# Backward attention by half sequences, early weight loads, a shared ring for the weight gradients, and one head of four of dS transposed on TensorE

## The chip, the cores and the metric

The kernel runs on one core of one Trainium2 chip. The metric is the device time of one execution in microseconds (us), the median of the timed runs. Where runs counted as slow (over 1.5% above the fastest of the same kernel), they are left out of the ratios.

Engines are called PE (TensorE matmul), PEld (its weight loads), DVE (VectorE), ACT (ScalarE), POOL (GpSimd) and SP (SyncE, used here only to issue DMAs). A name with a q, as in SPq, is that engine's DMA-issuing instructions. "PEclk" is the granted TensorE clock, 1.00 at full speed.

## The reference, cut to what matters

Forward and gradient of four residual layers over 2048 tokens of width 640: linear attention (A), sliding-window attention (B), A, B. Both have 32 heads of 20 channels. All A layers share weights, and all B layers do, so the weight gradients sum over two layers each.

```python
def _B_ref(x, wqkv, wo):
    B, S, D = x.shape
    H = 32; Dh = D // H; W = 256
    ...                                   # q, k, v from x @ wqkv
    scores = jnp.einsum("bhqd,bhkd->bhqk", q, k) * (Dh ** -0.5)
    mask = (idx[:, None] - idx[None, :] >= 0) & (idx[:, None] - idx[None, :] < W)
    p = _softmax(jnp.where(mask[None, None], scores, -1e9), axis=-1)
    o = jnp.einsum("bhqk,bhkd->bhqd", p, v)
    return (...)(o) @ wo                  # heads put back side by side

x = A_x
x = x + _A_ref(_layernorm(x), A_wqkv, A_wo)
x = x + _B_ref(_layernorm(x), B_wqkv, B_wo)
x = x + _A_ref(_layernorm(x), A_wqkv, A_wo)
x = x + _B_ref(_layernorm(x), B_wqkv, B_wo)
# outputs: x, and the gradients of A_x, A_wqkv, A_wo, B_wqkv, B_wo for a given grad_out
```

## The kernel before

The stages run one after another: forward; the first output gradient dO ("first dO"); backward attention of layer 3; then "B-to-A" (through layer 3's projections down into layer 2) and "A-to-B" (layer 2 into layer 1); the same three for layers 1 and 0; at last the weight gradients.

Backward attention works on units. A unit is one of 8 groups of four heads and one of 16 blocks of 128 queries, with up to three blocks of 128 keys. The order of PE's work is written by hand: step s of the loop works on parts of several units, so that PE need not wait for the exponential (ACT) and the product dS (DVE) of the unit just issued. dS has to be transposed for dq, which runs eight units later. All DMA transposes are issued by SP, the slab loads (q, k, v and dO of one head group) by ACT, and the stores by SP.

```python
def dma(self, out, in_, eng=None): (eng or self.nc.scalar).dma_start(...)   # ACT unless told (abridged)
def st(self, out, in_): self.dma(out, in_, self.nc.sync)                    # SP
def ld(self, out, in_): self.dma(out, in_, self.nc.gpsimd)                  # POOL
def tr(self, out, in_): self.nc.sync.dma_start_transpose(out=out, in_=in_)  # SP

def seg_attention_bwd(self, l):
    LAG = 8
    units = [(g, b) for g in range(G) for b in range(TT)]
    ...
        psl = self.pool(st, "atl", 2)          # slabs: this head group and the next
        pe = self.pool(st, "ate", 9)           # e, ds, dsT of nine units
        ps_sp = self.pool(st, "pss", 3, PSUM)  # three score buffers
        ps_o = self.pool(st, "pso", 2, PSUM)   # two accumulators
        ...
        def dscore(u, half, ps):
            ...                                # ds = score * e, two heads of four at a time, on DVE
            if half == 1:
                dsT_of[u] = pe.tile([P, 12, P], BF, name="dsT")
                self.tr(dsT_of[u][:, 0:4 * nkt, :], ds_of[u][:, 0:4 * nkt * P])   # all four heads
        ...
        for s in range(n + LAG):
            if s < n and units[s][1] == 6 and units[s][0] + 1 < G:
                load(units[s][0] + 1)          # seven slabs of 512 KB
            if s < n:
                expo(s, 0, scores(s, 0, "QT", "KT"))              # scores of heads 0, 1
            if 0 <= s - 3 < n:
                dscore(s - 3, 1, scores(s - 3, 1, "dOT", "VT"))   # dS scores of heads 2, 3
            key_products(s)                                       # dV and dK
            if s < n:
                expo(s, 1, scores(s, 1, "QT", "KT"))
            if 0 <= s - 2 < n:
                dscore(s - 2, 0, scores(s - 2, 0, "dOT", "VT"))
            if 0 <= s - LAG < n:
                dq(s - LAG)

def seg_B_to_A(self, l, acc, dqT):
    ...
        WT = self.load_w(pW, 1, "WT")     # DMA transposes of the weights, in each B-to-A
        WoT = self.load_w(pW, 0, "WoT")

def weight_grads(self, ls, out_dW, out_dWo):
    ...
        for kind, (srcs, width, dst) in enumerate(((self.hn_d, 480, out_dW), (self.o_d, HD, out_dWo))):
            with ExitStack() as s2:
                pW = self.pool(s2, "wg")          # left operands: closed and opened anew per kind
                pw = self.pool(s2, "wgw", 2)
                ...                               # load lhs of two layers, then rhs by columns, then matmuls
```

The softmax here doesn't subtract the row's maximum and nothing guards it: scores larger than these inputs give would overflow.

## Time and profile before

| | before |
|---|---|
| time | 2887.16 us, median of 2 (2881.89 and 2892.43) |
| profiled span | 2894.6 us, mean granted clock 0.757 |
| attention, layers 3 and 1, first to last exponential | 400.3 and 382.5 us |
| wait of PE before each B-to-A | 40.4 and 40.8 us |
| idle of PE before and within the weight gradients | 23.9 + 61.9 us |

The first view is the part of the profile page that cuts the span into 40 slices of 72 us, here of the kernel before. A digit is a busy share (or the clock) in tenths.

```profile
PE   7588997489987676778397996876866978896796
PEclk9789897688876655555598995555558979898898
DMA  6699884498884999999944669999995355835624
```

Where PEclk reads 5 and DMA reads 9, the kernel is in backward attention: slices 15 to 19 and 25 to 30, counted from 1 (slice 20 is mostly PE's wait before B-to-A). PE is never full there although it is the engine with the most work.

The next view gives busy times in chosen stretches of the kernel before: first the two attention stages, then the four holes of the weight gradients. The columns are the stretch, its length, busy us of PE, PEld, DVE, ACT and POOL with counts, the granted clock, the DMA share (the packets' time over the time of the 16 DMA engines; it passes 1 where packets overlap) and GB/s.

```profile
978.50:1378.70 400.20, 305.08 (x4172) 116.18 (x4171) 244.97 (x310) 228.84 (x375) 146.25 (x238) 0.50 1.12 201
1753.70:2136.20 382.50, 306.50 (x4173) 116.09 (x4171) 244.45 (x310) 229.28 (x375) 146.25 (x238) 0.50 1.13 211
2449.00:2473.00 24.00, 0.15 (x2) 0.00 (x0) 2.08 (x6) 1.45 (x3) 0.00 (x0) 0.61 1.04 324
2605.00:2625.00 20.00, 0.44 (x3) 0.00 (x0) 0.66 (x1) 0.00 (x0) 0.00 (x0) 0.58 0.96 353
2670.00:2692.00 22.00, 0.55 (x5) 0.18 (x2) 0.49 (x1) 0.00 (x0) 0.00 (x0) 0.57 0.96 355
2824.00:2845.00 21.00, 0.50 (x3) 0.21 (x3) 0.66 (x1) 0.00 (x0) 0.00 (x0) 0.56 0.98 352
```

In attention PE is busy for 305 of 400 us, at half clock throughout. In the holes PE does nothing while 352 to 355 GB/s arrive (324 in the first).

The view of waits of the kernel before, for PE, says for whom it stood: total us, times, longest.

```profile
PE acc L806 <- DMA dsT<-ds: 79.7, 29, 11.7
PE d L581 <- DMA WT_32780<-in_B_wqkv_dram: 40.8, 1, 40.8
PE d L581 <- DMA WT_21469<-in_B_wqkv_dram: 40.4, 1, 40.4
PE wg L971 <- DMA wg_r_36633<-dqkvT_117: 23.9, 1, 23.9
PE wg L971 <- DMA wg_r_37765<-dqkv_115: 21.6, 1, 21.6
```

The first line is the transposed dS arriving late. The timeline of the kernel before shows one such wait. PE (start, length, work, and in brackets the idle time before it and who ended it):

```profile
1187.79 0.50 PE L731 MATMUL sp<-KT,QT 32*128 32x384 bf16 x2
1187.80 0.50 PE L731 MATMUL sp<-VT,dOT 32*128 32x384 bf16 x2
1199.95 0.30 PE L806 MATMUL acc<-dsT,ksl 128*32 128x128 bf16 x4 [11.65 <-DMA dsT<-ds]
```

and, of the same view and kernel, SP's queue around it:

```profile
1154.78 2.67 SPq L136 DMA_TRANSPOSE dsT<-ds  x1
1157.54 4.02 SPq L127 DMA_DIRECT2D dqkvT_117<-dqkvT_g  x7
1161.66 38.98 SPq L136 DMA_TRANSPOSE dsT<-ds  x10
```

SP issues ten transposes back to back over 38.98 us, 3.9 us each, and dq waits.

Unit paces, worked out from the starts of the exponentials in the trace (us per unit, b = 0 to 15, then the sum), show where a group of heads loses time. This is head group 4 of layer 3, before:

```
2.9 2.6 2.1 5.8 14.2 5.0 1.5 4.5 1.5 2.8 2.6 2.6 2.6 4.1 2.3 2.4   = 59.4
```

Quiet units, those without a stall, take 2.6 us; this is called the quiet pace below. Units b = 3 to 7 stall. The middle groups take 48 to 59 us (layer 3) and 46 to 57 us (layer 1), the first and last 37 to 40 us.

### The profile page before, as it was taken

The page shows a single profiled execution, that of the slowest core. Times are in us where ns is not written, and L with a number is a line of the kernel's source. Part 1 is how long each engine was busy: PE and PEld are TensorE (multiplying, and loading weights), DVE is VectorE, ACT ScalarE, POOL GpSimd, SP SyncE. Part 2 cuts the span into 40 slices and gives each one's busy share as a digit, 9 for nine tenths or more (in the row PEclk, how much of TensorE's full clock was granted, in tenths as well). Part 3 has the DMA queues.
Part 4 walks back from the last instruction along what each step waited for, and adds up shares of the span by engine and source line. Part 5 has one row for each costly group of instructions (what it writes and reads, how often), then busy time and mean ns, then how long its engine had stood idle before and what let it go on. Part 6 is the DMA issues. An engine that isn't in the chain of part 4 may idle for free. (4 is left out here: it accounts for less than half of the span.)

```text
span 2894.6 us, 60635 instructions
## 1 busy us (share of the span) xinstructions
PE 2261.8 (78%) x24412; PEld 1255.8 (43%) x24412; DVE 1335.5 (46%) x2804; ACT 1297.4 (45%) x2339; POOL 852.0 (29%) x1310
## 2 busy tenths in 40 slices
PE   7588997489987676778397996876866978896796
PEld 5345554245544332233265762332324756344344
DVE  6445553344324665566285675664754845000000
ACT  4257676146765555556143665654642545000000
POOL 0124444125545433333243233332442311000000
PEclk9789897688876655555598995555558979898898
DMA  6699884498884999999944669999995355835624
GB/s 199 206 173 186 176 178 126 141 182 172 178 187 119 243 210 202 178 209 180 197 153 121 165 171 227 218 205 184 226 191 164 122 137 179 197 74 188 220 73 159
DMA packets 1001434, 507.72 MB, mean 175 GB/s; under 512 B 841920, under 2 KB 964800, under 8 KB 1000128
## 3 DMA queue, kind: packets, MB, share of 16 engines
q1 hardware_dynamic: 793152, 240.60, 47.2%
q10 hardware_dynamic: 194816, 216.04, 25.3%
q0 software_dynamic: 13184, 47.20, 5.4%
q8 instruction: 191, 3.13, 0.4%
q14 instruction: 91, 0.75, 0.1%
HBM read 173.41 MB, written 148.50 MB: 111 GB/s over the span
## 5 line engine op out<-in xcount | busy, mean ns | idle before, releaser
L764 DVE TENSOR_TENSOR ds<-sp,e 128x768 bf16<-128x768 f32 (+2 forms) x512 | 460.6, 907 | 315.3 <-PE sp L731 285.3
L745 ACT ACTIVATE e<-sp 128x768 bf16<-128x768 f32 (+2 forms) x512 | 389.2, 774 | 185.8 <-PE sp L731 166.8
L359 ACT ACTIVATE e<-s 128x768 bf16<-128x768 f32 (+2 forms) x512 | 373.9, 774 | 148.0 <-PE s L357 106.6
L749 POOL TENSOR_SCALAR_AFFINE_SELECT e<-e 128x512 bf16<-128x512 bf16 x256 | 163.1, 637 | 520.0 <-ACT e L745 272.9
L731 PE MATMUL sp<-KT,QT 32*128 32x384 bf16 (+2 forms) x1024 | 243.1, 477 | 57.7 <-ACT e L745 28.9
L362 POOL TENSOR_SCALAR_AFFINE_SELECT e<-e 128x512 bf16<-128x512 bf16 x256 | 163.4, 638 | 414.1 <-ACT e L359 410.7
L731 PE MATMUL sp<-VT,dOT 32*128 32x384 bf16 (+2 forms) x1024 | 245.3, 470 | 44.9 <-DVE ds L764 28.0
L975 DVE CAST wg_r<-wg 128x480 bf16<-128x480 f32 (+1 forms) x36 | 21.7, 602 | 417.0 <-PE wg L971 417.0
L977 ACT CAST wg_r<-wg 128x480 bf16<-128x480 f32 (+1 forms) x24 | 12.4, 515 | 422.8 <-PE wg L971 403.9
L806 PE MATMUL acc<-dsT,ksl 128*32 128x128 bf16 x2880 | 125.0, 304 | 84.0 <-DMA dsT<-ds 79.7
L357 PE MATMUL s<-ring 32*128 32x128 bf16 x2880 | 168.3, 236 | 26.2 <-ACT e L359 25.0
L583 ACT ACTIVATE dh_junk<-d 128x320 bf16<-128x320 f32 x128 | 56.2, 439 | 240.1 <-PE d L581 240.0
L365 POOL TENSOR_SCALAR_AFFINE_SELECT e<-e 128x512 bf16<-128x512 bf16 x224 | 143.9, 642 | 0.0
L581 PEld LDWEIGHTS <-dqkvT 128*128 128x128 bf16 x960 | 93.1, 100 | 116.4 <-issue 81.6
L357 PEld LDWEIGHTS <-ring 32*128 32x128 bf16 x2880 | 84.2, 98 | 135.9 <-issue 128.7
L753 POOL TENSOR_SCALAR_AFFINE_SELECT e<-e 128x512 bf16<-128x512 bf16 x224 | 142.8, 637 | 0.0
L731 PEld LDWEIGHTS <-dOT 32*128 32x128 bf16 x1024 | 76.9, 99 | 149.5 <-issue 145.0
L231 PEld LDWEIGHTS <-ln_hnT 128*128 128x128 bf16 x960 | 96.5, 107 | 92.4 <-DMA ln_hnT<-ln_hn 34.6
L218 DVE TENSOR_TENSOR car<-d,car 128x320 bf16<-128x320 f32 x128 | 62.2, 486 | 158.4 <-PE d L216 157.8
L378 PEld LDWEIGHTS <-e 128*128 128x128 bf16 x2880 | 103.8, 98 | 67.1 <-POOL e L365 37.1
L806 PEld LDWEIGHTS <-ksl 128*32 128x32 bf16 x2880 | 61.9, 121 | 163.1 <-issue 112.0
L731 PEld LDWEIGHTS <-QT 32*128 32x128 bf16 x1024 | 55.0, 100 | 177.1 <-issue 174.6
(774 smaller groups left out, 4608.1 us busy)
## 6 DMA issues: line engine op xcount, KB each, us to landing
qkvT_127<-ring ACTq DMA_DIRECT2D x16, 768.0 KB
qkvT_131<-ring ACTq DMA_DIRECT2D x16, 768.0 KB
dqkvT_117<-dqkvT_g SPq DMA_DIRECT2D x96, 80.0 KB
dqkvT<-dqkvT_117 POOLq DMA_DIRECT2D x4, 1920.0 KB, 14.1
dqkvT_116<-dqkvT_g SPq DMA_DIRECT2D x96, 80.0 KB
dqkvT<-dqkvT_116 POOLq DMA_DIRECT2D x4, 1920.0 KB, 13.5
dqkv_115<-dkv_t SPq DMA_DIRECT2D x16, 320.0 KB
dqkv_114<-dkv_t SPq DMA_DIRECT2D x16, 320.0 KB
```

Source lines behind the costliest of these rows:

```text
L231: nc.tensor.matmul(ps, lhsT=hnT[:, k, :], rhs=W[:, k, ci * HD:(ci + 1) * HD], start=(k == 0), stop=(k == self.DT - 1))
L357: nc.tensor.matmul(ps[:, j, i * P:(i + 1) * P], lhsT=ring[r0:r0 + HP, G + g, kt * P:(kt + 1) * P], rhs=ring[r0:r0 + HP, g, qs], start=True ...
L359: nc.scalar.activation(ev[:, 2 * half:2 * half + 2], ps[:, :, 0:nkt * P].rearrange("p h (i q) -> p h i q", q=P), ACT.Exp, scale=self.c_att)
L362: nc.gpsimd.affine_select(out=ev[:, :, nkt - 1, :], in_=ev[:, :, nkt - 1, :], compare_op=ALU.is_ge, fill=0.0, base=0, pattern=[[0, 4], [1, ...
L365: nc.gpsimd.affine_select(out=ev[:, :, 0, :], in_=ev[:, :, 0, :], compare_op=ALU.is_ge, fill=0.0, base=-1, pattern=[[0, 4], [-1, P]], chan ...
L378: nc.tensor.matmul(ov[:, (g % 4) * 4 + hh, :], lhsT=ev[:, hh, i, :], rhs=slabs[(k0 + i) % len(slabs)][:, c0:c0 + DH + 1], start=(i == 0), ...
L731: nc.tensor.matmul(ps[:, j, 0:nkt * P], lhsT=slabs[g][ta][r0:r0 + HP, b * P:(b + 1) * P], rhs=slabs[g][tb][r0:r0 + HP, k0 * P:(k0 + nkt) * P],
L745: nc.scalar.activation(ev[:, 2 * half:2 * half + 2], ps[:, :, 0:nkt * P].rearrange("p h (i k) -> p h i k", k=P), ACT.Exp, scale=c_att)
L749: nc.gpsimd.affine_select(out=ev[:, :, nkt - 1, :], in_=ev[:, :, nkt - 1, :], compare_op=ALU.is_ge, fill=0.0, base=0, pattern=[[0, 4], [-1 ...
L753: nc.gpsimd.affine_select(out=ev[:, :, 0, :], in_=ev[:, :, 0, :], compare_op=ALU.is_ge, fill=0.0, base=-1, pattern=[[0, 4], [1, P]], chann ...
L764: nc.vector.tensor_tensor(out=dv[:, hs], in0=ps[:, :, 0:nkt * P].rearrange("p h (i k) -> p h i k", k=P), in1=ev[:, hs], op=ALU.mult)
L806: nc.tensor.matmul(acc[HP * hh:HP * (hh + 1), j * P:(j + 1) * P], lhsT=tok("k", g, k0 + i, hh), rhs=dsT[:, hh * nkt + i, :], start=(i == 0 ...
```

## The change

Four things are intended:

1. Attention: slabs by half sequences (half as large, in a ring of three), one head of four of dS transposed on PE instead of by DMA, and a new order of PE's work to make room for it. The key products move behind the second scores.
2. WT and WoT for both B-to-A stages are transposed once, early, and kept.
3. The weight gradients' operands go through two shared rings (6 left tiles, 8 right tiles of half a sequence) that last over all four gradients. The first left tiles are loaded before the last A-to-B.
4. The copy of dK moves from DVE to ACT.

The diff also changes smaller things: ds and dsT have 8 and 7 buffers instead of 9, a score matmul that crosses the half-sequence boundary is split in two, and in the weight gradients SP instead of ACT issues the loads and the output projection comes first.

The diff, cut to its core (half-slab indexing and the rest of the weight-gradient code are cut):

```diff
-            psl = self.pool(st, "atl", 2)
-            pe = self.pool(st, "ate", 9)
+            psl = self.pool(st, "atl", 3)
+            po = self.pool(st, "ato", 2)
+            pe = self.pool(st, "ate")
 ...
-                    self.tr(dsT_of[u][:, 0:4 * nkt, :], ds_of[u][:, 0:4 * nkt * P])
+                    self.tr(dsT_of[u][:, 0:3 * nkt, :], ds_of[u][:, 0:3 * nkt * P])
+
+            def flip(u):
+                nb = span(units[u][1])[1]
+                tp = ps_o.tile([P, 1024], BF, name="acc")
+                for i in range(nb):
+                    nc.tensor.transpose(tp[:, i * P:(i + 1) * P], ds_of[u][:, (3 * nb + i) * P:(3 * nb + i + 1) * P],
+                                        self.ident)
+                dst = dsT_of[u][:, 3 * nb:4 * nb, :].rearrange("p i q -> p (i q)")
+                nc.vector.tensor_copy(dst, tp[:, 0:nb * P])
 ...
-                    nc.vector.tensor_copy(o, acc)
+                    nc.scalar.copy(o, acc)
 ...
             for s in range(n + LAG):
-                if s < n and units[s][1] == 6 and units[s][0] + 1 < G:
-                    load(units[s][0] + 1)
+                if pX is not None and s == TT:
+                    late = self.rinv[3][:, TT - 1, 0:1]
+                    self.WT_B = self.load_w(pX, 1, "WT", late)
+                    self.WoT_A = self.load_w(pX, 0, "WoT", late)
+                if s < n:
+                    g, b = units[s]
+                    if b == 2 and g > 0:
+                        load(g, 1)
+                    elif b == HT and g + 1 < G:
+                        load(g + 1, 0)
                 if s < n:
                     expo(s, 0, scores(s, 0, "QT", "KT"))
                 if 0 <= s - 3 < n:
                     dscore(s - 3, 1, scores(s - 3, 1, "dOT", "VT"))
-                key_products(s)
+                if 0 <= s - 4 < n:
+                    flip(s - 4)
                 if s < n:
                     expo(s, 1, scores(s, 1, "QT", "KT"))
                 if 0 <= s - 2 < n:
                     dscore(s - 2, 0, scores(s - 2, 0, "dOT", "VT"))
+                key_products(s)
                 if 0 <= s - LAG < n:
                     dq(s - LAG)
 ...
-            WT = self.load_w(pW, 1, "WT")
-            WoT = self.load_w(pW, 0, "WoT")
+            WT, WoT = self.WT_B, self.WoT_A
 ...
                 self.seg_B_to_A(l, acc, dqT)
+                if l == 1:
+                    right.close()
+                    pl = self.pool(right, "wgl", 6, side="right")
+                    lhs = self.wg_lhs((3, 1), 1, pl)
                 self.seg_A_to_B(l - 1, acc, dqT)
-        self.weight_grads((3, 1), self.out_dWB, self.out_dWoB)
-        self.weight_grads((2, 0), self.out_dWA, self.out_dWoA)
+        with right, ExitStack() as st:
+            pr = self.pool(st, "wgr", 8)
+            pw = self.pool(st, "wgo", 4)
+            pps = self.pool(st, "ps", 6, PSUM)
+            self.weight_grads((3, 1), 1, self.out_dWoB, lhs, pr, pw, pps)
+            self.weight_grads((3, 1), 0, self.out_dWB, self.wg_lhs((3, 1), 0, pl), pr, pw, pps)
+            self.weight_grads((2, 0), 1, self.out_dWoA, self.wg_lhs((2, 0), 1, pl), pr, pw, pps)
+            self.weight_grads((2, 0), 0, self.out_dWA, self.wg_lhs((2, 0), 0, pl), pr, pw, pps)
```

## The prediction

> **What bounds the kernel now (before, 2894.6 us span).** Stages from the windows view:
>
> - The two backward-attention stages (978-1402 and 1754-2158 us, 423 and 405 us) run at a granted TensorE clock of 0.50 throughout, PE busy 75-78%, DMA share 1.11. In quiet stretches one unit (a head group and a query block) takes 2.60 us: the timeline shows PE back to back (score pairs 0.5 us, dq 0.51, a key product 0.83). In six of eight head groups the units around b = 4-7 take 5-14 us, because PE waits for dS transposes (waits: "acc <- DMA dsT<-ds", 80 us over the kernel, single waits to 12 us). A middle group takes 46-59 us instead of about 38.
> - In 1130-1140 us the DMA records show 4096-byte slab-load packets taking 0.79 of the 16 engines; transposes (256-byte packets) fall to about 100 packets/us from 500-600. The Trainium skill, "DMA: Bandwidth & Descriptors", section on queues, rings and completion order, says each engine round-robins between queues by packet; this agrees.
> - Before each B-to-A stage PE stands 40.4 and 40.8 us, last released by the transposed weight WT.
> - Weight gradients (2449-2895 us) are a critical PE chain of 356 us with four holes of 20-24 us waiting for operands.
>
> **What the change does, costed.**
>
> 1. *Weight-gradient ring.* Operands load ahead, and the first left operands during A-to-B. The first hole shrinks to perhaps 15 us (2.6 MB must still land when the pool frees); the other three to about 6 us, because only two of four left tiles can be prefetched. Gain about 50 us. The 5.2-7.8 MB of early loads precede A-to-B's own weight transpose in the SP queue: about +8 us there.
> 2. *Early WT/WoT, once instead of twice.* The B-to-A start then waits for the dqkvT load (issued 6 us after the stage, 14 us to land): gain about 12 us each, 24 us. But the instruction order puts WT (75 blocks, about 16 us of transposing, as at 1402 us) on the SP queue in front of the WoT that the first dO stage waits for: that stage starts about 12 us later. They are not loaded during attention, as the code suggests. Net 12 us.
> 3. *Attention.* A quarter fewer transpose bytes, and loads as twice as many halves in 2 KB packets. Per middle group I estimate DMA work: transposes 38 -> 28 us, loads 14 us, stores 4 us: 55 -> 46 us. Most dsT waits should go. Against it PE gains three 128-column transposes per unit (0.106 us each at clock 0.5, plus a change of tiling mode: 0.35-0.45 us), at a place where the exp-to-dS loop leaves no slack: quiet pace 2.60 -> about 2.95 us, or 46-48 us a group, now also for the first and last groups (38 us before). DVE (a 384-column copy instead of half a 256-column one, net about +0.3 us a unit) and ACT stay below PE. "TensorE: Matmul & The Clock Gate", Part 4, says transposes do not count as activity, so I expect the clock to stay 0.50. Net: layer 3 about 20 us faster, layer 1 about 3 us.
>
> Sum: -50 +8 -12 -24 = about -80 us.
>
> **Predicted: 2807 us, 2735-2865 (8 in 10). Faster by over 2%: 0.70; within 2%: 0.26; slower: 0.04.**
>
> **What would show it.** Groups even at 45-50 us, PE busy near 95% in attention, unit pace 2.9-3.0 us, dsT waits below 25 us; attention stages 395-410 us each; first PE wait before B-to-A about 25-30 us; the first dO matmul about 12 us later; weight-gradient stage near 395 us.
>
> **What would make it wrong.** The clock rising above 0.50 in attention (large gain); flips, key products and dq sharing two PSUM buffers, so that PE waits for DVE and ACT copies (pace 3.2 us, attention slower); transposes still starving; early loads delaying A-to-B more.

## The result, and the profile after

The kernel after takes 2784.93 us, median of 2 runs (2777.49 and 2792.37). The ratio to the kernel before is 0.964, with a 95% interval from 0.958 to 0.971. Ratios in this document are the mean time of one kernel's fast runs over the mean of the other's of the same rounds, so they are not quite the ratio of the medians quoted. The profiled execution has a span of 2790.4 us at a mean clock of 0.776.

Lengths of the stages, worked out from the first and last matmuls and exponentials of each in the two traces:

| stretch | before | after | difference | predicted |
|---|---|---|---|---|
| start to the first dO matmul | 915.0 | 935.9 | +20.8 | +12 |
| attention layer 3, first to last exponential | 400.3 | 369.6 | -30.7 | -20 |
| its end to the first B-to-A matmul | 54.6 | 38.8 | -15.8 | -12 |
| attention layer 1 | 382.5 | 383.4 | +0.9 | -3 |
| its end to the first B-to-A matmul | 53.6 | 37.2 | -16.4 | -12 |
| gap before the last A-to-B | 39.2 | 48.6 | +9.4 | +8 |
| gap before the weight gradients | 23.9 | 9.6 | -14.3 | together -50 |
| PE idle within the weight gradients | 61.9 | 2.5 | -59.4 | |
| all else (PE's work in the weight gradients -7.6, small gaps elsewhere +8.9) | | | +1.3 | 0 |
| sum | | | -104.1 | -80 (rounded) |

PE's waits in the kernel after, from the same view as before (total, times, longest):

```profile
PE sp L752 <- ACT e L767: 40.5, 41, 5.5
PE d L588 <- DMA dqkvT<-dqkvT_116: 23.6, 1, 23.6
PE d L588 <- DMA dqkvT<-dqkvT_117: 23.2, 1, 23.2
PE d L545 <- DMA WoT_14005<-in_B_wo_dram: 22.5, 1, 22.5
PE wg L1039 <- DMA wg_r<-in_grad_out_dram: 9.6, 1, 9.6
```

No wait for a DMA of dsT is among the lines of this view any more. Before B-to-A PE now waits 23 us for the operand dqkvT instead of 40 us for the weight. A new wait of 22.5 us stands in the first dO stage, and one of 9.6 us is what remains before the weight gradients.

The same stretches as before in the kernel after: two attention stages, the gap before the weight gradients, the weight gradients.

```profile
1002.50:1372.00 369.50, 333.08 (x4622) 157.67 (x4622) 254.82 (x373) 252.10 (x434) 145.68 (x238) 0.54 0.99 187
1737.50:2120.90 383.40, 341.86 (x4622) 160.29 (x4622) 255.07 (x373) 252.84 (x435) 145.68 (x238) 0.51 0.97 179
2426.40:2436.10 9.70, 0.05 (x2) 0.05 (x2) 2.08 (x6) 1.45 (x3) 0.00 (x0) 0.62 0.50 143
2436.10:2787.10 351.00, 348.51 (x1920) 187.90 (x1920) 21.02 (x35) 12.33 (x24) 0.00 (x0) 1.00 0.62 173
```

The weight gradients are now solid: PE is busy 348.5 of 351.0 us at full clock. In attention PE is busy for 90% and 89% of the stage, and the clock is a little above 0.50.

The new wait of the first dO stage is a matter of the order in SP's queue. The timeline of SP, before:

```profile
909.26 3.69 SPq L136 DMA_TRANSPOSE WoT_14005<-in_B_wo_dram  x1
```

and after:

```profile
906.00 22.43 SPq L136 DMA_TRANSPOSE WT_15398<-in_B_wqkv_dram  x1
928.65 4.16 SPq L136 DMA_TRANSPOSE WoT_14005<-in_B_wo_dram  x1
```

The early WT, which the code asks for at step 16 of the attention loop, has reached SP's queue ahead of the WoT that the first dO stage needs. The value it is made to wait for (the reciprocal row sums of layer 3) is ready at that time, so the gate holds nothing back.

The left operands do the same to the last A-to-B. Its transpose of WT in SP's queue, before and after:

```profile
2330.29 12.39 SPq L136 DMA_TRANSPOSE WT_34858<-in_A_wqkv_dram  x1
2299.48 21.66 SPq L136 DMA_TRANSPOSE WT_36799<-in_A_wqkv_dram  x1
```

It takes 9.3 us longer, behind and beside four loads of left operands, and the transposes of v that PE waits for stand behind it.

Before the weight gradients, after the change, PE ends at 2426.4 us and starts again at 2436.1 us. SP's queue in between:

```profile
2425.40 5.16 SPq L127 DMA_DIRECT2D out_dram<-car  x2
2431.04 1.03 SPq L127 DMA_DIRECT2D wg_r<-in_grad_out_dram  x2
```

The first load of a right tile is issued 4.6 us into the gap, after the last two stores of the stage before, and PE starts 5.0 us later.

Unit paces of head group 4, layer 3, after (compare with the line of before):

```
2.5 3.1 3.0 3.5 3.6 2.3 2.3 3.0 3.0 2.9 3.0 3.0 3.0 3.0 3.0 2.8   = 46.8
```

Quiet units are slower than before (3.0 against 2.6), but none stalls in this group. In others small stalls are left at b = 1 and b = 9, just where the loads of another half slab stand in the program (the code asks for them at b = 2 and b = 8): up to 5.8 and 8.1 us in layer 1.

### The profile page after: what moved, and what is told of

It reads as the page before. It is cut to its first block, busy times and chain, and to the rows that moved or that the text cites. A ratio compares the mean times of both kernels' runs of the same rounds, so it can differ in the third digit from the quotient of the medians.

```text
span 2790.4 us, 63430 instructions
## 1 busy us (share of the span) xinstructions
PE 2321.5 (83%) x25388; PEld 1342.6 (48%) x25388; DVE 1356.2 (49%) x2932; ACT 1347.3 (48%) x2467; POOL 849.7 (30%) x1312
## 5 line engine op out<-in xcount | busy, mean ns | idle before, releaser
L366 ACT ACTIVATE e<-s 128x768 bf16<-128x768 f32 (+2 forms) x512 | 374.1, 774 | 151.7 <-PE s L364 106.1
L1039 PE MATMUL wg<-wg_r,wg_l 128*128 128x480 bf16 (+1 forms) x1920 | 348.5, 345 | 12.1 <-DMA wg_r<-in_grad_out_dram 9.6
L1039 PEld LDWEIGHTS <-wg_l 128*128 128x128 bf16 x1920 | 187.9, 98 | 172.6 <-issue 10.2
L1043 DVE CAST wg_o<-wg 128x480 bf16<-128x480 f32 (+1 forms) x36 | 21.7, 602 | 335.9 <-PE wg L1039 332.0
L588 PE MATMUL d<-WT_15398,dqkvT 128*128 128x320 bf16 x960 | 144.2, 305 | 46.8 <-DMA dqkvT<-dqkvT_116 23.6
L1045 ACT CAST wg_o<-wg 128x480 bf16<-128x480 f32 (+1 forms) x24 | 12.3, 514 | 339.5 <-PE wg L1039 303.1
L588 PEld LDWEIGHTS <-dqkvT 128*128 128x128 bf16 x960 | 92.8, 99 | 81.9 <-issue 47.3
```

The source lines that it names most:

```text
L366: nc.scalar.activation(ev[:, 2 * half:2 * half + 2], ps[:, :, 0:nkt * P].rearrange("p h (i q) -> p h i q", q=P), ACT.Exp, scale=self.c_att)
L588: nc.tensor.matmul(ps, lhsT=dT[k], rhs=WT[:, k, cs], start=(k == 0), stop=(k == self.QTT - 1))
L1039: nc.tensor.matmul(ps, lhsT=lhs[i][:, tt, m * P:(m + 1) * P], rhs=rhs[i][:, tt, :], start=(i == 0 and tt == 0), stop=(i == len(parts) - 1 ...
```

## The experiments

Twelve kernels were run, each with one profile and three rounds beside the kernel before on the same chip. All gave correct results, the three with useless work included. The kernel before had a median of 2894.5, 2876.0, 2870.0 and 2892.2 us in the four calls. It differs by chip, so totals are compared by the ratio.

Stage lengths are each from a single profile. How far they can be trusted is seen where the attention code is the same: after, experiment 3 and experiment 4 have 369.6, 379.0 and 368.3 us in layer 3, and 383.4, 375.0 and 373.3 us in layer 1. Differences of 10 us between single stages are therefore not read as effects unless a second sign goes with them. A kernel named "after minus" or "before plus" is that kernel with the edit shown and nothing else.

The theory at the start was the one predicted: the PE transposes cost the slower quiet pace, and fewer DMA transposes take the stalls away. The rivals: the new order of PE's work does one or both; or half slabs do.

### 1. After, without the PE transposes

```diff
-                    self.tr(dsT_of[u][:, 0:3 * nkt, :], ds_of[u][:, 0:3 * nkt * P])
+                    self.tr(dsT_of[u][:, 0:4 * nkt, :], ds_of[u][:, 0:4 * nkt * P])
 ...
-                if 0 <= s - 4 < n:
-                    flip(s - 4)
```

> The changed kernel with the PE transposes undone: all four heads of dS go through the DMA again, the half-sequence slabs stay. Theory A (the DMA work per group was the bound of the old attention stage, and the PE transposes pay for themselves by taking a quarter of it away): quiet pace back at 2.6 us a unit, but middle groups back at 49-54 us with dsT waits, first and last groups 38 us; each attention stage, first exp to last exp, 375-395 us. Theory B (the smaller, earlier slab loads did the work, and the PE transposes cost): quiet pace 2.6 us, middle groups 40-44 us, stage 330-345 us. On the clock: if the PE transposes are what lifts the granted clock above 0.50 for stretches of the changed kernel's attention, it is 0.50 throughout here; if slab loads or order did it, the stretches at 1.0 stay.

Measured: 2817.57 us, ratio 0.971 (0.963 to 0.979). Attention takes 385.7 and 395.4 us, middle groups 48 to 54 us, and the quiet pace is still about 3.0 us. The stretches of the two stages:

```profile
997.30:1383.00 385.70, 285.23 (x4274) 130.38 (x4274) 224.67 (x250) 244.42 (x434) 146.02 (x238) 0.50 1.08 208
1745.70:2141.00 395.30, 285.77 (x4274) 130.66 (x4274) 224.91 (x250) 243.82 (x434) 146.03 (x238) 0.50 1.09 203
```

PE has 48 and 56 us less work than in the kernel after (285 against 333 and 342 us), and yet the pace is the same. PE's waits of this run say why:

```profile
PE sp L752 <- ACT e L767: 156.1, 176, 5.2
```

This line was 40.5 us after and 37.0 us before (51 times). With the key products moved behind the second scores, PE reaches those scores earlier than the exponential frees their buffer. The transposes in the kernel after fill time that would otherwise be this wait. So the cause I gave for the pace of 3.0 us is wrong: the order sets it, as experiment 5 confirms. PE's waits for dsT, 79.7 us before, are 7.9 us in this run, although all four heads are on DMA.

### 2. Before, with the PE transposes, their order and the dK copy on ACT

```diff
+ flip(), called as in the kernel after; DMA transposes of three heads; dK copy on ACT
-                key_products(s)
+                if 0 <= s - 4 < n:
+                    flip(s - 4)
                 if s < n:
                     expo(s, 1, scores(s, 1, "QT", "KT"))
                 if 0 <= s - 2 < n:
                     dscore(s - 2, 0, scores(s - 2, 0, "dOT", "VT"))
+                key_products(s)
```

> The kernel before with only the PE transposes of one head of four (and the dK copy on ACT and the order of PE that belong to them); full-sequence slabs, no ring, no early weights. Theory A: quiet pace 3.0 us, dS transposes 28 us a group instead of 38, so stalls at b = 4-7 shrink but do not vanish, because the 4 KB slab packets still crowd the transposes out: middle groups 48-53 us, stage about 385-395 us. Theory B (loads are everything): stalls as before on top of a 3.0 us pace, middle groups 57-62 us, stage about 430 us. Clock: stretches above 0.50 should appear here too if the transposes cause them.

Measured: 2869.36 us, ratio 0.987 (0.980 to 0.995). Attention takes 374.1 and 369.3 us; quiet pace 3.0 us, middle groups 45.1 to 48.7 us. This is with whole slabs. The kernel after has 369.6 and 383.4 us, so its half slabs bring nothing to attention that these profiles show.

### 3. After, with gates that hold the early loads back

```diff
             WoT = self.load_w(pW, 1, "WoT")                       # in the first dO stage
+            self.WT_B = self.load_w(pX, 1, "WT", WoT[:, 0, 0:1])
+            self.WoT_A = self.load_w(pX, 0, "WoT", WoT[:, 0, 0:1])
 ...
             WT = self.load_w(pW, 0, "WT")                         # in the last A-to-B
+            if pl is not None:
+                self.lhs0 = self.wg_lhs((3, 1), 1, pl, WT[:, 0, 0:1])
```

Each early load now has to follow the weight that the running stage needs, by a copy of one element of that weight into its target.

> The changed kernel with two loads put behind the ones that are needed first: WT_B and WoT_A wait for the WoT of the first dO stage, and the left operands of the weight gradients wait for A-to-B's WT. Theory: the 20.8 us delay of the first dO matmul and the 9.4 us longer start of the last A-to-B stage are both queueing on the DMA behind transfers nobody needs yet. First dO matmul back at about 915 us (from 936), gap before the last A-to-B stage back at about 39 us (from 48.6), all else unchanged: 28-30 us faster than the changed kernel, about 2755 us. Rival (the DMA is simply full there, so the order does not matter): the time comes back within the first dO stage or at the start of the weight gradients, total gain under 10 us.

Measured: 2773.67 us, ratio 0.956 (0.949 to 0.962). The first dO matmul comes at 911.3 us, 24.6 us earlier than after. The gap before the last A-to-B shrinks by 10.3 us to 38.3 us, but that stage grows from 98.5 to 112.0 us. The gate on the weight works. The one on the left operands only moves their cost.

The start of a run varies by chip and run, so the first dO matmul is best judged over all runs. In the five kernels with the order of before it came at 904 to 918 us (mean 911.1), in the five with the order of after at 923 to 936 us (mean 929.5), and in the four with the gate at 910 to 917 us (mean 912.1).

### 4. After, with rings of four

```diff
-                    pl = self.pool(right, "wgl", 6, side="right")
+                    pl = self.pool(right, "wgl", 4, side="right")
 ...
-            pr = self.pool(st, "wgr", 8)
+            pr = self.pool(st, "wgr", 4)
```

Four left and four right tiles are one gradient's operands, so nothing can be prefetched for the next one.

> The changed kernel with the rings cut to one set: 4 right tiles instead of 8 and 4 left tiles instead of 6, so nothing loads ahead across a boundary. Theory (the gain of 74 us in the weight-gradient part is loading ahead): holes of 8-20 us return at the three boundaries between products and, as there is now only one set of right tiles, smaller ones at each column block: stage 40-90 us longer than the changed kernel's 361 us. Rival (the gain comes from the new order, out-projection first, and the early left operands): stage within 15 us of 361 us.

Measured: 2842.11 us, ratio 0.980 (0.972 to 0.987). PE idles 66.1 us within the weight gradients, as before the change (61.9), and the time from the last A-to-B matmul to the last weight-gradient matmul is 430.6 us against 360.7 us after. So the prefetching is the gain, not the half tiles, the shared pool, the new order of the gradients or the loads from SP by themselves, all of which this run keeps. The first gap is 4.7 us here against 9.6 us.

### 5. Before, with only the key products moved

```diff
                     dscore(s - 3, 1, scores(s - 3, 1, "dOT", "VT"))
-                key_products(s)
                 if s < n:
                     expo(s, 1, scores(s, 1, "QT", "KT"))
                 if 0 <= s - 2 < n:
                     dscore(s - 2, 0, scores(s - 2, 0, "dOT", "VT"))
+                key_products(s)
```

All four heads still go through DMA.

> The kernel before with one edit: the key products of a step are issued on PE after the second pair of score matmuls instead of before it. No PE transposes, no halves. New theory C (formed after the run without PE transposes kept the 3.0 us pace): the pace of the changed kernel is set by the order of PE, not by the transposes, because nothing is left to fill the 1.4 us between a score matmul and the dS matmul that needs its PSUM buffer. Then quiet pace goes from 2.60 to 3.0 us here, with PE waiting for ACT's exp before the dS matmul many times. Rival (the dK copy on ACT or the split matmuls slowed it): pace stays 2.60 us. The stage total should move less than the pace (400 and 383 us before), since it was held by DMA.

Measured: 2866.67 us, ratio 0.995 (0.990 to 1.000). In its profile attention takes 378.4 and 367.8 us, about as in experiment 2; quiet pace 2.9 to 3.0 us, and the middle groups are 47.3 us, flat, but for one stall of 14.6 us. PE waits once for dsT, against 79.7 us in 29 waits before:

```profile
PE acc L806 <- DMA dsT<-ds: 10.2, 1, 10.2
```

The two stages of this run:

```profile
972.60:1350.90 378.30, 284.36 (x4148) 126.31 (x4146) 245.26 (x310) 223.75 (x374) 145.74 (x238) 0.50 1.10 214
1724.60:2092.40 367.80, 284.12 (x4148) 126.38 (x4146) 245.45 (x310) 224.01 (x374) 145.74 (x238) 0.50 1.09 220
```

This refutes the step of the prediction that put the DMA work of a group at 55 us for four heads: here it fits into 47.3 us. The estimate had been taken from a queue that was backed up. It also shows that most stalls go without any transpose on PE.

One caution. Experiment 5 ran on a chip on which the kernel before is faster too (2876.0 us), and its profiled run was the fastest of four (2851 us; the others 2862 to 2874). By the timed ratio the order alone gained 0.5%, by stage lengths 37 us. Experiment 2 gained 1.3% and 39 us. The two intervals overlap (0.990 to 1.000, and 0.980 to 0.995). Whether the PE transposes add up to about 1% of their own in this structure is therefore not settled.

### 6. After, with the key products back and the transposes last

```diff
-                if 0 <= s - 4 < n:
-                    flip(s - 4)
+                key_products(s)
                 if s < n:
                     expo(s, 1, scores(s, 1, "QT", "KT"))
                 if 0 <= s - 2 < n:
                     dscore(s - 2, 0, scores(s - 2, 0, "dOT", "VT"))
-                key_products(s)
                 if 0 <= s - LAG < n:
                     dq(s - LAG)
+                if 0 <= s - 4 < n:
+                    flip(s - 4)
```

> The changed kernel with PE's order put back (key products before the second pair of scores, then dq) and the PE transposes last in the step, so that they lie between dq and the next scores. Theory C: the transposes then sit in the wait for exp and cost nothing: quiet pace 2.6-2.65 us, first and last groups 37-39 us instead of 43-44 for the last, middle groups 44-47 us (now DMA, which I put at about 46 us), attention stages 340-360 us each against 370-383, total 2740-2765 us. Rival (PE time itself is the bound, so the transposes' 0.4 us adds wherever they stand): quiet pace 3.0 us, total within 10 us of the changed kernel.

Measured: 2723.08 us, ratio 0.945 (0.940 to 0.949), against 0.964 for the change itself. Attention takes 352.1 and 342.9 us, quiet pace about 2.77 us, middle groups 43 to 49 us. The key products are again between the two scores, so the exponential has time to finish; the pace is 0.17 us above that of before, where theory C had at most 0.05. The clock was at full for 47.7 and 74.1 us of the two stages.

### 7. After, with the slab loads issued by POOL

```diff
-                    self.dma(r[n], sv["qkvT"][:, i * G + g, h * HT * P:(h + 1) * HT * P])
+                    self.ld(r[n], sv["qkvT"][:, i * G + g, h * HT * P:(h + 1) * HT * P])
 ...   (the same for the other slabs)
```

The question was what stalls the kernel after at b = 1 and b = 9. ACT's timeline of the kernel after shows a suspect: a slab load stands in ACT's instruction stream and waits, and the exponential behind it comes 6 us late.

```profile
1951.57 0.81 ACT L767 ACTIVATE e<-sp 128x768 bf16<-128x768 f32 x1 [0.22 <-PE sp L752]
1958.08 0.33 ACTq L127 DMA_DIRECT2D KT<-qkvT_127  x1
1958.45 0.81 ACT L767 ACTIVATE e<-sp 128x768 bf16<-128x768 f32 x1 [6.08 <-DMA dsT<-ds]
```

> The changed kernel with the slab loads of attention issued by POOL instead of ACT. Theory D (the residual stalls of 2-5 us at b = 1 and b = 9 are ACT's queue standing at a slab load that waits for a buffer or for a DMA semaphore it shares with the transposes, so that exp comes late): these units fall to 3.0-3.5 us, ACT waits on dsT DMAs from 13-16 us a stage to under 3, middle groups 45.5-46.5 us, stages about 360-365 us, total 15-25 us less than the changed kernel. Rival (the stalls are late dS transposes, slowed by the slab packets whoever issues them): the stalls stay within 20% or move to PE waiting for dsT, total within 8 us.

Measured: 2749.33 us, ratio 0.956 (0.951 to 0.961). The units b = 1 and b = 9 of the middle groups are at 2.4 to 3.0 us, these groups at 43.2 to 48.6 us, attention 358.3 and 360.6 us. ACT's waits for dsT in the two stages go from 13.6 and 16.3 us to at most 0.6 us. The theory holds: the stalls were loads that waited in ACT's stream. (The first groups are longer than after, 43.6 and 40.9 against 37.5 us, with new stalls in them that were not looked into.) The Trainium skill, "DMA: Bandwidth & Descriptors", section "Issuing engines are not separate DMA queues", says that issuing from several engines only saves the sequencer's time to initiate the DMA, usually small. That is not what counted here: the time that the instruction waits holds up the compute behind it, 6.08 us in the lines above.

### 8. The gate of 3, the order of 6 and the loads of 7 together

```diff
+ the gate on WT and WoT (experiment 3, without the one on the left operands)
+ key products back, transposes last (experiment 6)
+ slab loads by POOL (experiment 7)
```

> The changed kernel with three edits that do not touch each other: WT_B and WoT_A behind the first WoT (20 us in the gates run), PE's order put back with the transposes last, slab loads issued by POOL. If theories C and D both hold the sum is about -20 (first dO) -40 (pace) -20 (stalls) = 2700-2720 us, and what bounds attention is then the DMA at about 45 us a middle group. If C holds and D does not: about 2730 us. If neither: about 2768 us.

Measured: 2706.58 us, ratio 0.941 (0.935 to 0.946). Attention takes 347.5 and 343.1 us. The parts do not add: new stalls of 4 to 9 us appear, most of them at b = 4 and 5. PE waits 59.0 us for dsT in this run, in 26 waits; before most of the long ones the 12 stores of a finished half slab stand between the transposes in SP's queue, 3, 2 and 7 together. That may be why, but no run tests it. The clock is at full for 101.7 and 150.8 us of the two stages:

```profile
976.80:1324.30 347.50, 294.63 (x4651) 138.32 (x4648) 254.81 (x373) 247.75 (x436) 200.62 (x343) 0.65 1.04 202
1682.20:2025.20 343.00, 277.45 (x4648) 133.33 (x4648) 252.33 (x373) 244.47 (x435) 200.47 (x343) 0.72 1.06 205
```

### 9. Before, with the scores of heads 0 and 1 issued twice

Experiment 5 raised a question: does the new order itself help the transposes, or is it just the slower pace? To tell them apart, the kernel before is slowed by useless work in its old order. The result stays right, since the repeat overwrites the same scores.

```diff
+                    for _ in range(2 if (half, ta) == (0, "QT") else 1):
                         nc.tensor.matmul(ps[:, j, 0:nkt * P], lhsT=...)
```

> The kernel before, order of PE unchanged, with the two score matmuls of heads 0 and 1 issued twice (same values written again): a pure slowing of PE by some 0.4 us a unit, in the order that stalled. It tells two readings of the reordered run apart, which got faster although its quiet pace fell from 2.60 to 3.0 us. Theory P (pace: at 2.60 us the transpose queue never catches up, so a slab load stops PE at once; at 3.0 us it runs ahead by several units and the load is absorbed): quiet pace 2.9-3.1 us, DMA stalls at b = 4-7 mostly gone, middle groups 46-49 us, stages 365-380 us against 400 and 383: slower work, shorter or equal stage. Rival O (the order itself, key products before the second scores, made the stall): stalls of 5-14 us stay on top of the slower pace, stages 420-440 us.

Measured: 2879.09 us, ratio 1.006 (0.996 to 1.015). The quiet pace was only 2.66 us, as the repeat hid in a wait, so the experiment did not do what it was for. The stalls stayed (5 to 10 us), and attention took 373.0 and 397.8 us. Inconclusive.

### 10. Experiment 8 with five useless PE transposes per unit

```diff
-                for i in range(nb):
-                    nc.tensor.transpose(tp[:, i * P:(i + 1) * P], ds_of[u][:, (3 * nb + i) * P:(3 * nb + i + 1) * P],
-                                        self.ident)
+                for i in range(8):
+                    c = 3 * nb + i % nb
+                    nc.tensor.transpose(tp[:, i * P:(i + 1) * P], ds_of[u][:, c * P:(c + 1) * P], self.ident)
```

The rising clock of 6 and 8 was against the prediction. If the transposes raise it, more of them must raise it further.

> The combination run with useless PE transposes added: 8 instead of 3 per unit, the extra ones into a part of the PSUM tile that nobody reads. Theory H (full-array transposes count as activity and lift the clock: all runs with them had stretches at 1.0 in attention, all four without had none): the granted clock is 1.0 for most of both stages (over 250 us each, against 102 and 151), quiet pace 2.1-2.4 us, stages 320-335 us in spite of the added work, total 2660-2690 us. Rival (transposes do not count; the stretches came from denser score matmuls): time at 1.0 stays or falls, each unit pays up to 0.5 us, pace about 3.1 us, stages 375-395 us, total about 2780 us.

Measured: 2709.97 us, ratio 0.945 (0.934 to 0.956). Attention takes 347.5 and 343.7 us, the same as in experiment 8. The clock is at full for 252.0 and 253.7 us:

```profile
984.70:1332.10 347.40, 282.05 (x5278) 163.75 (x5275) 253.72 (x373) 241.20 (x435) 200.55 (x343) 0.86 1.04 203
1686.50:2030.20 343.70, 282.45 (x5282) 163.09 (x5283) 254.86 (x373) 241.40 (x436) 200.32 (x342) 0.87 1.05 204
```

PE did some 630 more instructions per stage, and was busy for about as long as in experiment 8 (282 and 282 us against 295 and 277), as it ran at a clock of 0.86 and 0.87 instead of 0.65 and 0.72. The stage did not move: the useless work was free. PE is busy for 81% of the stage, so its work alone does not set the length.

That 8 transposes in place of 3 raise the clock is seen in the timed runs too: their mean clock over the whole kernel is 0.87 to 0.88 here and 0.81 to 0.83 in experiment 8.

### 11. Experiment 8 with two heads of four transposed on PE

```diff
-                    self.tr(dsT_of[u][:, 0:3 * nkt, :], ds_of[u][:, 0:3 * nkt * P])
+                    self.tr(dsT_of[u][:, 0:2 * nkt, :], ds_of[u][:, 0:2 * nkt * P])
 ...
-                for i in range(nb):
+                for i in range(2 * nb):        # and the indices to match
```

> The combination run with two heads of four transposed on PE instead of one. Half of the dS bytes leave the DMA for good; PE has 6 useful full-array transposes a unit, DVE copies 768 columns instead of 384 (about 0.55 us, DVE about 2.5 us a unit). If theory H holds the clock is at 1.0 longer than in the combination run and the pace is set by DVE at about 2.5 us, groups 36-40 us, stages 310-330 us, total 2640-2680 us. If PE transposes do not lift the clock: pace about 3.1 us, stages 370-385 us, total about 2770 us.

Measured: 2630.01 us (2619.48 to 2633.51), ratio 0.920 (0.912 to 0.928). Attention takes 311.2 and 305.3 us, quiet pace 2.3 to 2.4 us, middle groups 37.7 to 42.4 us, clock at full for 239.7 and 256.1 us.

Beside experiment 10 this run also says which of its two effects did it, the smaller share of the DMA or the higher clock. Experiment 10 has about the same time at full clock, with three heads on DMA instead of two, and gained nothing over experiment 8. PE's waits for dsT, first in experiment 10, then here:

```profile
PE acc L840 <- DMA dsT<-ds: 55.5, 37, 6.2
PE acc L840 <- DMA dsT<-ds: 0.2, 1, 0.2
```

So at this pace three heads on DMA hold the stage up, and the clock alone does not help. What two heads on DMA would bring at half clock was not run.

This is the best version: it beats the kernel before by 8%. By its ratio (0.920 against 0.964) it beats the kernel after by about 4.5%. It was run at another time.

### 12. Before, with the dS scores of heads 2 and 3 issued twice

The repair of experiment 9: the same kind of useless work, at a place where it can't hide.

```diff
+                    for _ in range(2 if (half, ta) == (1, "dOT") else 1):
                         nc.tensor.matmul(ps[:, j, 0:nkt * P], lhsT=...)
```

Theory: any slower pace of PE takes the stalls away. Rival: the order of the work does it.

> The question of the last slowed run again, whose repeated score matmuls hid in a wait (quiet pace 2.66 us, not 3.0): the kernel before, order of PE unchanged, now with the dS score matmuls of heads 2 and 3 issued twice, which stand after that wait, so that they must lengthen the step by about 0.4 us. Theory P (a slower quiet pace lets the transposes run ahead, and the slab load is absorbed): quiet pace 2.95-3.05 us, no unit above 5 us after the first group, middle groups 47-49 us, stages 370-385 us. Rival O (the old order makes the stalls): quiet pace 2.95-3.05 us and still units of 5-14 us at b = 4-7, middle groups 53-60 us, stages 410-440 us.

Measured: 2843.94 us, ratio 0.983 (0.975 to 0.990), so the kernel is faster with useless work in it. Attention takes 361.6 and 360.6 us, 39 and 22 us less than before. Unit paces of head group 4, layer 3:

```
3.2 2.5 2.6 3.2 3.0 2.8 3.0 2.6 3.0 2.7 2.9 2.9 2.9 2.9 2.9 2.9   = 46.1
```

The quiet pace went from 2.60 to 2.92 us and no unit of the middle groups stalls (one of 5.9 to 6.5 us is left in each first group, as before). PE's list of waits has no line for dsT any more. The two stages:

```profile
972.90:1334.50 361.60, 337.97 (x4425) 121.52 (x4423) 245.91 (x310) 230.66 (x375) 145.67 (x238) 0.50 1.09 224
1708.10:2068.70 360.60, 338.17 (x4421) 121.55 (x4421) 245.81 (x310) 230.68 (x375) 145.63 (x238) 0.50 1.08 225
```

PE is busy 32 us longer per stage than before and the stage is shorter. The DMAs move the same slabs and transposes in less time (224 and 225 GB/s against 201 and 211). From the trace, SP was issuing for 0.94 and 0.92 of the two stages before and for about 0.8 here. So SP's queue of transposes was near its limit at a pace of 2.60 us and has slack at 2.92 us. The theory holds for this run. The rival falls: the order in this run is the old one. That SP's queue had slack is read from these shares and not varied by itself.

The stage lengths say 61 us in all, but the profiled run is the fastest of the four (2828.77; the others 2834 to 2858 us), and stalled stages scatter: experiment 9, nearly the kernel before, has 373.0 us where before has 400.3. By the ratio of all runs the gain is 1.7%, about 50 us.

What stays open is why the DMA engines get less done when the queue is backed up. Before, in the 8 us from 1184 us on, the trace has 175 transpose packets per us with 0.086 MB/us of loads, and from 1192 us on 126 packets with 0.109 MB/us. In experiments 5 and 12 such slices of 8 us near by, with 0.13 MB/us of loads, have between 172 and 605 packets, so bad slices occur there too, but pass. No run separated the causes.

## Why the prediction was right or wrong

The direction and the total were right: 2807 us with a range of 2735 to 2865 us was predicted, 2784.93 us measured. For the weight gradients and the early weights the mechanism was right and sizes were off. For attention it was partly luck: the two terms that were set off against each other, the DMA work saved and the cost of the transposes, were both wrong. Point by point:

- **Weight gradients, -50 predicted, -74 measured.** The mechanism was right: operands load ahead (without prefetching, in experiment 4, the time from the last A-to-B matmul to the last weight-gradient matmul is 70 us longer again). The size was off. I expected holes of about 6 us to remain and the first one to be 15 us. They measured 2.5 us in all and 9.6 us. The step that failed is "2.6 MB must still land": these are the four right tiles of a column block, but PE starts before all of them are there. In the gap of 9.7 us only 1.4 MB moved in all (143 GB/s), about two tiles of half a sequence at 0.66 MB each, and 4.6 us of it passed before the first of these loads was issued. The holes before were another matter, as all operands had to be loaded there, at 352 to 355 GB/s. The Trainium skill, "DMA: Bandwidth & Descriptors", section "Bandwidth", gives about 358 GB/s per core when both cores of an HBM domain stream, and 425 GB/s for a large load of one core alone; the trace is near the first figure, and whether another core was loading it does not show.
- **B-to-A starts, -24 predicted, -32 measured.** The mechanism was right: PE waits 23.2 and 23.6 us for dqkvT, where I had 25 to 30 us in mind.
- **First dO, +12 predicted, +20.8 in the pair of traces.** The mechanism, WT in front of WoT in SP's queue, was right and is shown by the queue and by experiment 3. Over all runs the delay is 18.4 us (929.5 less 911.1). The mis-sized term was the transpose of WT, for which I took 16 us and which holds SP for 22.43 us there.
- **Last A-to-B, +8 predicted, +9.4 measured.** Right, the mechanism too: the transpose of WT there holds SP for 21.66 us instead of 12.39, and with the left operands held back (experiment 3) the gap is 38.3 us again.
- **Quiet pace, 2.95 predicted, about 3.0 measured; right number, wrong cause.** The prediction gave the PE transposes as the cause. Experiment 1 has none and keeps the pace; experiment 5 has only the new order and gets it. PE's wait for the exponential (156.1 us in experiment 1 against 37.0 us before) is what took its place.
- **"A quarter fewer transpose bytes ... Most dsT waits should go": right outcome, wrong cause for most of it.** The dsT waits did go. But experiments 5 and 12 have all four heads on DMA, and after the first head group the stalls go there too, all but one. In 12 only useless work that slows the pace was added. The term of "55 -> 46 us" of DMA work per group is the step that failed: it was read off a backed-up queue. A whole group takes 47.3 and 46.1 us in these two runs, so its DMA work for four heads is at most that. Fewer bytes do matter once the pace is faster: experiments 10 and 11 have about the same clock, and with two heads on DMA instead of three the stages fall from 347.5 and 343.7 to 311.2 and 305.3 us.
- **Attention as a whole, about -20 and -3 predicted, -30.7 and +0.9 measured.** Close, though not for the reasons predicted, and a single profile is good to about 10 us. The middle groups take 46.8 to 52.9 us, where 46 to 48 was predicted. In the profiles the order alone gives as much in attention as the whole change: -21.9 and -14.7 us in experiment 5. What the change has in addition partly cancels: the kernel after has waits at b = 1 and 9 that experiment 7 takes out (11 and 23 us of the stages), and its PE transposes make up for some of that (the stages are 16 and 12 us longer without them in experiment 1).
- **"PE busy near 95% in attention": 90% and 89% measured.** Part of what is missing is the stalls at b = 1 and b = 9: without them, in experiment 7, PE is busy for 331 of 358.3 us and 333 of 360.6 us, 92% of both. The rest was not traced to a cause.
- **"I expect the clock to stay 0.50": wrong.** I took this from the Trainium skill, "TensorE: Matmul & The Clock Gate", Part 4, which says that transposes do not count as PE activity in the same way. In the kernel after the clock was at full for 30.8 and 10.2 us of the two stages (in experiments 3 and 4, with the same attention code, for 10.2 and 6.8 and for 47.8 and 13.7 us). In the five runs without PE transposes there (before, 1, 5, 9 and 12) it was never at full. With about eight transposes per unit it was at full for 252.0 and 253.7 us. I did name a rising clock among what could make the prediction wrong; its effect in the kernel after was not measured apart.

## What to carry to other kernels

When a producer outruns a shared queue, ask first what its pace is worth: here useless matmuls that slowed the quiet pace by 12% made the attention stages of the profiles 6 and 10% shorter, and a service time read while a queue is backed up is not the cost of the work in it. A load in the instruction stream of a compute engine costs the time it waits (6.08 us in one case here), not only the time it takes to issue, so put loads that may wait on an engine with nothing urgent behind them. An early load has to be held back by something that is ready only after what the running stage needs, and its place in the queue has to be looked up in the trace, not in the code.

## What the Trainium skill lacked or had wrong

- "TensorE: Matmul & The Clock Gate", Part 4, says that the full clock does not engage for transposes on PE, as they do not count as busy in the same way. Here they raise it: 0 us at full clock in an attention stage without them, 30.8 and 10.2 us with three per unit after, 101.7 and 150.8 us in the denser experiment 8, and 252.0 and 253.7 us in experiment 10, which is experiment 8 with five more per unit. The transposes are also the only matmuls of these stages that use all 128 by 128 of the array. Which of the two matters is not told apart. The trace records them as matmuls with the identity; whether the mode that the page means was on, it does not show.
- The same page, Part 1, says that the clock is at half or full and changes by windows of about 3.4 us of activity. The clock records agree with the two states and the window (stretches of 3.4, 6.8, 10.2 and 13.7 us). But the page does not say that matmuls on part of the array can keep PE busy without releasing the clock: in experiment 12 PE is busy for 338 of 361.6 us with tiles of 32 by 128 and 128 by 32, and the clock stays at 0.50 throughout.
- "DMA: Bandwidth & Descriptors", section "Issuing engines are not separate DMA queues", counts only the time to initiate a DMA. It lacks the time that the instruction waits in a compute engine's stream; that a semaphore wait happens on the issuing sequencer stands elsewhere on that page, but no page says what it costs the compute behind it. ACT stood 6.08 us in one case, and moving the loads to POOL took 11 and 23 us out of the attention stages.
- The section "Queues, rings and completion order" of that page says that each DMA engine takes turns between queues by packet. The prediction used it for transposes starving beside loads, and the trace is in line with it, though the turns themselves are not to be seen: from 1128 to 1136 us of the kernel before, transposes fall to 96 packets per us, with loads taking 0.71 of the engines, from 426 in the 8 us before. No page says that a slower producer can shorten a stage by keeping such a queue from backing up: 2.60 to 2.92 us per unit, and 39 and 22 us less per stage.
